# Fused sigmoid attention and ReGLU FFN: down weights in two loads with a transpose between them, long VectorE jobs behind the token pairs' joins, PSUM banks freed ahead of the token sums

## The chip, the cores and the metric

The kernel runs on one core of one Trainium2 chip. The metric is device time in microseconds (us). A run whose granted TensorE clock or time marks it as disturbed would be called slow. The granted TensorE clock that is listed with a run is its mean over the run, as a share of full speed. This mean also counts the end of the run, where TensorE has nothing left to do: in the profile of the kernel before, its last product ends at 405.11 us, and from 407.99 us to the end at 409.83 the clock is 0.50 with no work in it, which costs nothing.

## The reference

```python
# q, k, v: (8 batches, 12 heads, 448 tokens, 64), float32
scores = scale * np.matmul(q, k.transpose(0, 1, 3, 2)) - np.log(S)
attn = 1.0 / (1.0 + np.exp(-scores))                 # sigmoid, no softmax
x = np.matmul(attn, v)                               # then heads to columns: (3584, 768)
gate = np.maximum(x @ w_gate, 0.0)                   # w_gate, w_val: (768, 1536)
val = x @ w_val
out = gate * val @ w_out                             # w_out: (1536, 768), out float32
```

## The kernel before

TensorE is the engine in demand (busy 95% of the span; VectorE comes next with 69%). While it makes scores (`qk`) and attention outputs (`pv`) of batch b, the feed-forward work of earlier batches is mixed in between. Inputs of batches from 2 on come in by GpSimd's DMA queue, are relaid by VectorE (`rel`) and transposed by DMA on SyncE's queue (`qkT<-rel`). A later batch's scores cannot start before that transpose has landed: batch 3's last one is issued at 95.22 us and takes 15.9 us to land, and the scores that read it start at 111.16.

All down products, and the gate and value products from batch 2 on, are made by a seven-product scheme on two blocks of tokens (a token pair) or two batches: VectorE forms sums of the operands, TensorE makes seven products instead of eight, VectorE and ScalarE join them. A token pair of the down projection looks like this (abridged; comments are mine). In the profiles `wo` is the down weights, `T` and `S` the sums of weights and tokens, `hT` the transposed hidden activations, `u` and `y` PSUM banks in which TensorE leaves products, `ysb` the joined output, `PT` the sigmoid's output:

```python
    def weight_sums(i):                      # once, on the down weights wo = [[B11, B12], [B21, B22]]
        sub(*((T1, B12, B11), (T2, B22, T1), (B12, B22, B12), (T4, B21, T2))[i])

    def token_sums(g, p):                    # ahead of the pair
        nc.vector.tensor_tensor(out=S1, in0=A21, in1=A22, op=AOP.add)
        sub(S2, S1, A11)

    def more_token_sums(g, p):               # inside the pair
        sub(S4, A12, S2)
        sub(A21, A11, A21)                   # S3, for the fifth product; in the profile "hT<-hT"

    def down_pair(g, p, beside, then, last, first_copy):
        ...
        b, a, c = bank("u"), bank("y11"), bank("y12")        # three PSUM banks of a ring of 8
        product(b, A11, B11)
        first_copy(y1[:, lo], b)             # VectorE, or ScalarE once attention is over
        product(a, A12, B21)
        beside()                             # jobs of the step, then more_token_sums
        plus(y1[:, lo], a)
        product(b, S2, T2, False)            # adds onto b: waits for first_copy
        scaled_act(y1[:, hi], b)
        product(c, S1, T1)
        scaled_act(y2[:, hi], c)
        product(b, S3, T3, False)            # the fifth product
        plus(y2[:, hi], b)
        product(c, S4, B22, False)
        plus(y1[:, hi], c)
        store(...)
        then()                               # sums of the next piece of work
        product(b, A22, T4, False)
        scaled_act(y2[:, lo], b)
```

The two halves of the down weights are loaded together, behind a `hold`: GpSimd copies two elements of a transposed tile, so whatever it issues next waits for that transpose (in the profile the copy runs at 91.59 us, after 16.56 us of idle time that the transpose ended, and the loads are issued from 92.04 on).

```python
    def load_o():
        for i in range(2):
            cs = slice(i * NFC // 2, (i + 1) * NFC // 2)
            nc.gpsimd.dma_start(wo[:, cs, :], moe_w_out.rearrange("(c p) m -> p c m", p=P)[:, cs, :])

    def hold(b, g):
        nc.gpsimd.tensor_copy(gate[0:1, :], qkT_tiles[(b, g)][0:1, 0, 0:2])
    ...
        elif b == 2:
            hooks = {
                3: [(0, lambda: (dma_transposes(3, 0), dma_transposes(3, 1), hold(3, 1), load_o()))],
                5: [(0, lambda: (dma_transposes(3, 2), gate_sums(0, 2), gate_sums(2, 4)))],
            }
```

Of the kernel before, what the change touches and what calls it, by code (L numbers as in the profile page):

```python
# [17 lines left out]
def kernel(  # L18
# [10 lines left out]
    nc = tc.nc  # L29

    B, H, S, D = q.shape
# [3 lines left out]
    P = 128  # L35
# [123 lines left out]
    load_v(1)  # L159
    load(1, 2, 3, "kq")  # L160

    def load_o():
        for i in range(2):
            cs = slice(i * NFC // 2, (i + 1) * NFC // 2)
            nc.gpsimd.dma_start(
                wo[:, cs, :], moe_w_out.rearrange("(c p) m -> p c m", p=P)[:, cs, :]
            )

    qkT_tiles = {}
    xT_tiles = {}  # L170
# [245 lines left out]
    def more_token_sums(g, p):  # L416
        A11, A12, A21, A22 = token_blocks(g, p)
        S1, S2, S4 = sums["y"]
        sub(S4, A12, S2)
        sub(A21, A11, A21)  # L420
# [80 lines left out]
        sub(B12, B22, B12)  # L501
        sub(T4, B21, T2)

    def gv_units(g, fs, beside, first_copy, final):
        x1, x2 = xT_tiles[2 * g], xT_tiles[2 * g + 1]
        T1, T2, T4 = (late["X"][:, i] for i in range(3))
        B11, B21, T3, B22 = x1[:, 0:HD], x1[:, HD:NDC], x2[:, 0:HD], x2[:, HD:NDC]
        b, a, c = ([bank(nm) for _ in fs] for nm in ("u", "g1", "g2"))
        later((4, 5, 6, 7, 2, 3))
        gs = [[gsbp.tile([P, S], FP32, tag="gsb", name="gsb") for _ in range(3)] for _ in fs]  # L510
        sets = []
        for u, f in enumerate(fs):
            us, cols = slice(u * P, (u + 1) * P), slice(f * P, (f + 1) * P)
            S1, S2, S4 = (t[:, :, us] for t in sums["w"])
            sets.append((
                wg[:, 0:HD, cols], wg[:, HD:NDC, cols], wv[:, HD:NDC, cols],
                S1, S2, wv[:, 0:HD, cols], S4,
            ))
        del sums["w"]

        def product(ps, i, W, first=True):
            for u in range(len(fs)):
                products([(ps[u], S, HD, sets[u][i], W, first)])

        def copy(i, ps, by=nc.scalar.copy):
            for u in range(len(fs)):
                by(gs[u][i][:], ps[u][:, 0:S])  # L527

        def plus(i, ps):
            for u in range(len(fs)):  # L530
                nc.vector.tensor_tensor(  # L531
                    out=gs[u][i][:], in0=ps[u][:, 0:S], in1=gs[u][i][:], op=AOP.add
                )

        product(b, 0, B11)
        copy(0, b, first_copy)
        product(a, 1, B21)
        beside()
        plus(0, a)
        product(b, 4, T2, False)  # L540
        copy(1, b)
        product(c, 3, T1)
        copy(2, c)
        product(b, 5, T3, False)
        plus(2, b)
        product(c, 6, B22, False)
        plus(1, c)
        product(b, 2, T4, False)

        def finish(evens):  # L550
            for even in evens:
                for u in range(len(fs)):
                    if even:
                        gated(g, fs[u], 0, S, gs[u][0], b[u])
                    else:
                        gated(g, fs[u], S, S, gs[u][1], gs[u][2])

        if final == "even":
            finish((True,))
            prepare()  # L560
            return lambda: finish((False,))
        if final == "odd":
            finish((False,))
            prepare()
            finish((True,))
        else:
            finish((True, False))

    gv_queue = deque()

# [91 lines left out]

    work = deque()

    pending = []

    def push_group(g):
        if g > 0:
            work.extend([("w", g, (f, f + 1)) for f in range(0, NFC, 2)])
# [2 lines left out]
    def prepare():  # L672
        if work:
            kind, g, i = work[0]
            if kind == "w":
                unit_sums(g, i)
            elif kind == "y":
                token_sums(g, i)

    def next_work(jobs=(), alone=False):  # L680
        kind, g, i = work.popleft()

        def beside():
            while pending:
                pending.pop()()
            for job in jobs:
                job()

        if kind == "y":
            down_pair(  # L690
                g, i, lambda: (beside(), more_token_sums(g, i)), prepare, not work,
                scaled_act if alone else scaled,
            )
        else:
            first_copy = nc.scalar.copy if alone else nc.vector.tensor_copy
            if work[0][0] == "w":
                gv_units(g, i, lambda: (prepare(), beside()), first_copy, None)
            else:
                rest = gv_units(g, i, beside, first_copy, ("even", "odd")[g % 2])
                if rest:  # L700
                    pending.append(rest)

    ffn_mix(1, [(1, lambda: both(1, 0))])
    for b in range(1, B):
        if b == 1:
            cuts, pv_at = (0, 3, 6, 9, 13, 17, 21), {3: (0, 2), 5: (1, 2)}
        elif b == 2:
            cuts, pv_at = (0, 4, 7, 11, 14, 18, 21), {0: (-1, 2), 2: (0, 2), 4: (1, 2)}
        else:
            cuts, pv_at = (0, 4, 8, 12, 16, 21), {0: (-1, 2), 2: (0, 2), 4: (1, 2)}  # L710
        count = len(cuts) - 1
        hooks = {}
        if b == 1:
            mix = (3, 3, 3, 3, 3, 2)
            hooks = {
                1: [(1, lambda: both(1, 1))],
                3: [(1, lambda: both(1, 2))],
                4: [(3, lambda: dma_transposes(2, 0))],
                5: [(2, late_loads)],
            }  # L720
        elif b == 2:
            mix = (2, 2, 1, 1, 2, 1)
            hooks = {
                3: [(0, lambda: (dma_transposes(3, 0), dma_transposes(3, 1), hold(3, 1), load_o()))],
                5: [(0, lambda: (dma_transposes(3, 2), gate_sums(0, 2), gate_sums(2, 4)))],
            }
            open_late()
        elif b == 3:
            mix = (1, 1, 1, 0, 0)
            hooks = {  # L730
                0: [(0, lambda: (gate_sums(4, 6), gate_sums(6, 8)))],
                1: [(0, lambda: weight_sums(0))],
                2: [(0, lambda: (weight_sums(1), prepare()))],
            }
        else:
            mix = (0,) * count
        for m in range(count):
            jobs = []
            for i, (g, c) in enumerate(order[cuts[m] : cuts[m + 1]]):
                if m in pv_at and i == pv_at[m][1]:  # L740
                    if m == 0:
                        pv_finish(b - 1)
                        if b == 2:
                            push_group(0)
                    else:
                        pv_group(b, pv_at[m][0])
                qk_unit(b, g, c)
            if m == 0 and b > 1 and b != 3:
                jobs.append(lambda: dma_transposes(b, 2))
            if b == 3 and m == count - 2:  # L750
                jobs.append(lambda: (weight_sums(2), weight_sums(3)))
            elif b == 4 and m == 2:
                jobs.append(lambda: (gate_sums(8, 10), gate_sums(10, 12)))
            elif b == 3 and m == count - 1:
                jobs.append(lambda: (dma_transposes(4, 0), dma_transposes(4, 1)))
            elif 0 <= m - count + 2 and 3 < b < B - 1:
                jobs.append(lambda: dma_transposes(b + 1, m - count + 2))
            if b == 1:
                if m == 0:
                    load(2, 0, 1, "kq")  # L760
                    load(2, 1, 2, "kq")
                    load(2, 2, 3, "kq")
            elif m == 0 and b + 1 < B:
                if b == 3:
                    jobs.append(lambda: hold(3, 2))
                jobs.append(lambda: (load(b + 1, 0, 3, "kq"), load_v(b + 1)))
            if b % 2 and b > 2:
                if m == count - 1:
                    push_group(b // 2)
                    jobs.append(lambda: (batch_sums_t1(b // 2), batch_sums(b // 2, (0, 1))))  # L770
                    if b == B - 1:
                        jobs.append(lambda: (pv_finish(b), batch_sums(b // 2, (1, HD))))
            elif b > 3 and m == 0:
                jobs.append(lambda: batch_sums(b // 2 - 1, (1, HD)))
            if mix[m]:
                for job in jobs:
                    job()
                ffn_mix(mix[m], hooks.get(m, ()))
            else:
                next_work(jobs)  # L780
    while work:
        next_work((), True)


# [28 lines left out]
```

## Time and profile before

| | before |
|---|---|
| time, median of 4 runs | 411.29 us (411.04 to 412.12) |
| profiled span | 409.8 us |
| TensorE busy | 389.6 us |
| TensorE's waits for the last transpose of batch 3 | 4.4 us, once |
| TensorE's waits for VectorE's hT (S3) | 6.9 us in six pairs |
| mean granted clock | 0.994 in the profile, 0.990 to 0.996 over all runs |

The lines that carry the argument are in the prediction below. One more view is needed, the stretches of TensorE's clock. Its columns are the stretch and its length, then busy time and count of TensorE, its weight loads, VectorE, ScalarE and GpSimd, then the granted clock, the DMA share and GB/s:

```profile
107.62:111.03 3.41, 0.00 (x0) 0.00 (x0) 2.15 (x3) 0.89 (x3) 0.00 (x0) 1.00 0.51 66
111.03:114.44 3.41, 3.28 (x16) 1.38 (x17) 0.47 (x2) 1.85 (x4) 2.48 (x4) 0.50 0.21 11
```

A stretch of 3.41 us without any TensorE work is followed by one of the same length at clock 0.50, in which 3.28 us of work were done at half speed (six down matmuls took 2.10 us at 112.05, and 1.15 at 118.28). The two drops of the clock in this profile, at 111.03 and 407.99 us, are 87 times 3.413 us apart, so both lie on one grid of such windows. Work is compared with the clock below in windows of that length, cut at the drop of each profile, which lies elsewhere in each: in two profiles of the changed kernel at 112.17 and at 113.24 us.

### The profile page before, as it was taken

What the parts mean: (1) busy time and instruction counts of PE and PEld (TensorE: products, weight loads), DVE (VectorE), ACT (ScalarE), POOL (GpSimd) and SP (SyncE); (2) the same over time, 40 slices, a digit from 0 to 9 for tenths busy, and PEclk for the clock granted to TensorE, in tenths of its full rate; (3) what the DMA queues carried; (4) which work ended last, traced back from release to release, by engine and by line L of the source; (5) the groups of instructions that cost most, each with busy time, mean ns of one, the idle gap of its engine ahead of it and who ended that gap; (6) DMA issues with size and microseconds to landing.
All of it is one profiled execution on the core that took longest, in us unless ns stands there. A gap on an engine that the chain in (4) does not pass through costs nothing. (4 is left out here: it accounts for less than half of the span.)

```text
span 409.8 us, 8697 instructions
## 1 busy us (share of the span) xinstructions
PE 389.6 (95%) x3476; PEld 216.2 (53%) x3476; DVE 281.3 (69%) x570; ACT 229.9 (56%) x482; POOL 49.3 (12%) x74
## 2 busy tenths in 40 slices
PE   8999999999598999999999899999999899999995
PEld 3668775444244554554455445455455455555563
DVE  2443445344567789999756789999785779887662
ACT  5946777779634465655556455655645534433221
POOL 8643302301020300003000030000000000000000
PEclk9999999999999999999999999999999999999999
DMA  9999995999799791235916598022202220000235
GB/s 145 198 199 204 204 131 94 198 159 155 124 166 204 149 234 20 46 46 67 179 41 161 124 155 170 2 45 47 46 2 78 78 77 0 2 1 2 77 91 142
DMA packets 67257, 43.69 MB, mean 107 GB/s; under 512 B 35856, under 2 KB 63760, under 8 KB 67216
## 3 DMA queue, kind: packets, MB, share of 16 engines
q0 software_dynamic: 29200, 23.33, 37.3%
q1 hardware_dynamic: 37584, 19.24, 22.1%
q10 hardware_dynamic: 432, 0.56, 0.5%
q8 instruction: 27, 0.44, 0.4%
q14 instruction: 14, 0.11, 0.1%
HBM read 47.19 MB, written 11.01 MB: 142 GB/s over the span
## 5 line engine op out<-in xcount | busy, mean ns | idle before, releaser
L188 ACT ACTIVATE PT<-qk_ps 128x448 f16<-128x448 f32 (+3 forms) x318 | 150.9, 593 | 59.3 <-PE qk_ps L233 59.0
L385 PEld LDWEIGHTS <-S 128*128 128x128 f16 x576 | 56.1, 98 | 46.3 <-issue 0.4
L233 PE MATMUL qk_ps<-qkT 64*64 64x448 f16 (+2 forms) x756 | 50.6, 339 | 6.1 <-DMA qkT<-rel 4.4
L428 ACT ACTIVATE ysb<-u 128x384 f32<-128x384 f32 x32 | 15.7, 490 | 63.3 <-PE u L385 63.1
L385 PEld LDWEIGHTS <-hT 128*128 128x128 f16 x312 | 29.6, 99 | 31.6 <-DVE hT L376 9.7
L527 ACT COPY gsb<-u 128x448 f32<-128x448 f32 x48 | 25.6, 533 | 31.7 <-PE u L385 30.5
L531 DVE TENSOR_TENSOR gsb<-g,gsb 128x448 f32<-128x448 f32 x72 | 41.5, 616 | 0.1
L320 DVE SCALAR_TENSOR_TENSOR hT<-gate_sb,v_ps 128x256 f16<-128x256 f32 (+2 forms) x36 | 14.6, 420 | 37.9 <-ACT gate_sb L343 21.0
L185 DVE TENSOR_SCALAR xT<-pv_ps 128x448 f16<-128x448 f32 (+2 forms) x53 | 27.8, 566 | 16.1 <-PE pv_ps L251 15.5
L251 PE MATMUL pv_ps<-PT,v 64*64 64x448 f16 (+2 forms) x756 | 37.1, 329 | 1.0 <-issue 1.0
L385 PE MATMUL u<-wo,hT 128*128 128x384 f16 x156 | 30.7, 335 | 7.0 <-DVE hT L376 6.9
L233 PEld LDWEIGHTS <-qkT 64*64 64x64 f16 x756 | 20.1, 106 | 31.0 <-issue 17.3
L334 PE MATMUL g_ps<-xT,wg 128*128 128x256 f16 (+2 forms) x216 | 33.5, 292 | 0.1
L334 PE MATMUL v_ps<-xT,wv 128*128 128x256 f16 (+2 forms) x216 | 33.3, 291 | 0.0
L531 DVE TENSOR_TENSOR gsb<-u,gsb 128x448 f32<-128x448 f32 x36 | 21.4, 624 | 15.6 <-PE u L385 15.6
L385 PEld LDWEIGHTS <-wv 128*128 128x128 f16 x216 | 21.1, 98 | 19.8
L385 PEld LDWEIGHTS <-wg 128*128 128x128 f16 x216 | 20.3, 98 | 20.6 <-issue 3.0
L251 PEld LDWEIGHTS <-v 64*64 64x64 f16 x756 | 21.9, 107 | 12.0 <-issue 1.9
L110 POOL DMA_DIRECT2D k<-in_k_dram x14 | 10.9, 779 | 120.0 <-DVE rel L216 112.6
L334 PEld LDWEIGHTS <-wg 128*128 128x128 f16 x216 | 18.5, 97 | 11.5 <-issue 5.0
L334 PEld LDWEIGHTS <-wv 128*128 128x128 f16 x216 | 20.1, 98 | 7.6 <-DMA wv<-in_moe_w_val_dram 0.2
L385 PE MATMUL u<-xT,wg 128*128 128x448 f16 x108 | 23.5, 354 | 0.1
(71 smaller groups left out, 523.9 us busy)
## 6 DMA issues: line engine op xcount, KB each, us to landing
out_dram<-ysb SPq DMA_DIRECT2D x53, 192.0 KB, 3.0
k<-in_k_dram POOLq DMA_DIRECT2D x5, 672.0 KB, 9.3
q<-in_q_dram POOLq DMA_DIRECT2D x5, 672.0 KB, 13.3
v<-in_v_dram POOLq DMA_DIRECT2D x8, 336.0 KB, 13.3
v<-in_v_dram POOLq DMA_DIRECT2D x16, 168.0 KB, 13.3
wo<-in_moe_w_out_dram POOLq DMA_DIRECT2D x2, 1152.0 KB, 12.9
k<-in_k_dram POOLq DMA_DIRECT2D x8, 224.0 KB, 10.4
q<-in_q_dram POOLq DMA_DIRECT2D x6, 224.0 KB, 11.3
```

The lines of the kernel that those rows point to most:

```text
L110: nc.gpsimd.dma_start(t16[:, xs, cs], rows_of(src, b)[:, xs, cs])
L185: nc.vector.tensor_scalar(out=xT, in0=src, scalar1=XSCALE, scalar2=None, op0=AOP.mult)
L188: nc.scalar.activation(PT_ap, ps_ap, AF.Sigmoid, bias=sig_bias, scale=qk_scale)
L233: nc.tensor.matmul(out_of(hh)[o : o + 64, :], qkT[rows, c, cols], qkT[rows, NCH + c0 : NCH + c1, cols], start=True, stop=True, tile_positi ...
L251: nc.tensor.matmul(ps[hh][64 * r : 64 * r + 64, 0:qn], v16[rows, 2 * g + hh, c * D : (c + 1) * D], pieces[c][rows, hh, :], start=(c == 0), ...
L320: nc.vector.scalar_tensor_tensor(out=dst[:, f, a - d : z - d], in0=gate_sb[:, a - o : z - o], scalar=0.0, in1=val[:, a - o : z - o], op0=relu,
L334: nc.tensor.matmul(ps[-1][:, 0:qn], wt[:, dc, f * P : (f + 1) * P], xT_tiles[b][:, dc, q0 : q0 + qn], start=(dc == 0), stop=(dc == NDC - 1),)
L385: nc.tensor.matmul(ps[:, 0:n], A[:, k_, :], W[:, k_, :], start=(first and k_ == 0), stop=(k_ == kn - 1), skip_group_check=True,)
L428: nc.scalar.activation(o, ps[:, 0:HM], AF.Copy, scale=OUT_SCALE)
L527: by(gs[u][i][:], ps[u][:, 0:S])
L531: nc.vector.tensor_tensor(out=gs[u][i][:], in0=ps[u][:, 0:S], in1=gs[u][i][:], op=AOP.add)
```

## The change

Its intent has three parts. **Loads:** the last transpose of batch 3 shall not queue among 2.3 MB of down weights (where it took 15.9 us to land), so its relayout runs earlier, the first half of the weights is loaded ahead of it and the second half behind it. The hold that stood ahead of batch 4's inputs moves along with it. Of the weight sums, the first two that need the second half move behind the token sums. **Jobs:** relayouts and batch sums no longer stand ahead of the pair's own sums and joins in VectorE's queue. **Banks:** at the end of a gate/value unit, the gating that empties two PSUM banks comes ahead of the other half's gating and of the token sums, and nothing is deferred any more.

```diff
-    def load_o():
-        for i in range(2):
-            cs = slice(i * NFC // 2, (i + 1) * NFC // 2)
+    def load_o(i):
+        cs = slice(i * NFC // 2, (i + 1) * NFC // 2)
 ...
-    def gv_units(g, fs, beside, first_copy, final):
+    def gv_units(g, fs, beside, first_copy, then, split):
 ...
-        if final == "even":
-            finish((True,))
-            prepare()
-            return lambda: finish((False,))
-        if final == "odd":
-            finish((False,))
-            prepare()
-            finish((True,))
+        if split:
+            finish(False)
+            then()
+            finish(True)
         else:
-            finish((True, False))
+            finish(True)
+            finish(False)
+            then()
 ...
             down_pair(
-                g, i, lambda: (beside(), more_token_sums(g, i)), prepare, not work,
-                scaled_act if alone else scaled,
+                g, i, lambda: (more_token_sums(g, i), run(jobs)),
+                lambda: (run(behind), prepare()), not work, scaled_act if alone else scaled,
             )
 ...
-                3: [(0, lambda: (dma_transposes(3, 0), dma_transposes(3, 1), hold(3, 1), load_o()))],
-                5: [(0, lambda: (dma_transposes(3, 2), gate_sums(0, 2), gate_sums(2, 4)))],
+                3: [(0, lambda: (dma_transposes(3, 0), dma_transposes(3, 1), hold(3, 1), load_o(0)))],
+                5: [
+                    (1, lambda: (dma_transposes(3, 2), hold(3, 2), load_o(1))),
+                    (0, lambda: (gate_sums(0, 2), gate_sums(2, 4))),
+                ],
 ...
-                2: [(0, lambda: (weight_sums(1), prepare()))],
+                2: [(0, lambda: (prepare(), weight_sums(1), weight_sums(2)))],
 ...
-                jobs.append(lambda: (weight_sums(2), weight_sums(3)))
+                jobs.append(lambda: weight_sums(3))
 ...
-                if b == 3:
-                    jobs.append(lambda: hold(3, 2))
 ...
-                    jobs.append(lambda: (batch_sums_t1(b // 2), batch_sums(b // 2, (0, 1))))
+                    (jobs if b == B - 1 else behind).append(
+                        lambda: (batch_sums_t1(b // 2), batch_sums(b // 2, (0, 1)))
+                    )
 ...
-                jobs.append(lambda: batch_sums(b // 2 - 1, (1, HD)))
+                behind.append(lambda: batch_sums(b // 2 - 1, (1, HD)))
```

## The prediction

> **What bounds the kernel now.** I read the head of the page first, then the list of waits of TensorE alone, then the timelines of TensorE, VectorE and the DMA queues where those waits lie. The page says that TensorE works 95% of the span and the next engine 69%:
>
> ```profile
> PE 389.6 (95%) x3476; PEld 216.2 (53%) x3476; DVE 281.3 (69%) x570; ACT 229.9 (56%) x482; POOL 49.3 (12%) x74
> ```
>
> The change removes no matmul, so what it can win lies in the 20.2 us in which TensorE does nothing (409.8 less 389.6), and in matmuls that run at a reduced clock. The waits of TensorE (who waited for whom: us in total, times, longest):
>
> ```profile
> PE u L385 <- DVE hT L376: 6.9, 6, 1.7
> PE qk_ps L233 <- DMA qkT<-rel: 4.4, 1, 4.4
> ...
> PE qk_ps L233 <- DVE hT L320: 0.7, 2, 0.5
> ```
>
> The single wait of 4.4 us is for the last DMA transpose of batch 3. TensorE's timeline (start, us, what, idle before):
>
> ```profile
> 106.17 0.57 PE L233 MATMUL qk_ps<-qkT 64*64 64x448 f16 x8
> 111.16 0.96 PE L233 MATMUL qk_ps<-qkT 64*64 64x448 f16 x8 [4.42 <-DMA qkT<-rel]
> 112.05 2.10 PE L385 MATMUL u<-wo,hT 128*128 128x384 f16 x6
> ...
> 118.28 1.15 PE L385 MATMUL u<-wo,hT 128*128 128x384 f16 x6 [1.00 <-DVE hT L376]
> ```
>
> Read the durations too: six down matmuls take 2.10 us at 112.05 and 1.15 at 118.28. Windows of the same trace give a granted clock of 0.50 from 111.03 to 114.44 and 1.00 on both sides. So the wait also costs about half of 3.3 us at half clock, 1.6 us. Why the transpose is late, from DMA issues: it is issued at 95.22 and takes 15.9 us to land, where the two before it took 4.1 and 4.5. From 95 to 107 the queue is full of the two down-weight loads (1152 KB each, issued together at 92.04); from 99 to 107 the transpose's queue moves 834 small packets beside their 907[...], 104 a microsecond. Undisturbed, from 86.5 to 91, it moves 3639, some 810 a microsecond; one transpose has about 1800.
>
> The six waits of 6.9 us stand in the second half of a token pair, for the difference hT that VectorE makes for the fifth product. VectorE's timeline in the second pair shows why:
>
> ```profile
> 126.88 0.85 DVE L376 TENSOR_TENSOR X<-xT 128x1344 f16<-128x1344 f16 x1
> ...
> 128.68 0.55 DVE L376 TENSOR_TENSOR S<-hT,S 128x768 f16<-128x768 f16 x1
> 129.15 0.55 DVE L376 TENSOR_TENSOR hT<-hT 128x768 f16<-128x768 f16 x1
> ```
>
> The relayouts (rel) and batch sums (X) stand ahead of it in the queue. I measured pairs from first matmul to the next block: an undisturbed one takes 6.92 us (213.37 to 220.28). The pairs at 112.05, 124.02, 135.24, 222.99 and 233.36 take 9.26, 9.01, 7.98, 8.17 and 7.98; the one at 319.89 takes 9.97, of which 1.5 is another product. Lastly, from pv to the down pair at 205.35 takes 3.06 us where 1.81 is normal (182.89 to 184.70): the score matmuls wait for two PSUM banks that VectorE empties only after the token sums.
>
> [...]
>
> **Part 1, the loads.** The order of instructions shows that TensorE, ScalarE and SyncE keep their sequences; GpSimd gets the second load behind a copy that waits for the last transpose; VectorE's two relayout copies move ahead of one gating pair (hT/aside). They can then run at 90.97 instead of 94.47, end at 91.7, and the transpose is issued at about 91.75. Its first packets follow about 1.1 us after (85.30 to 86.4 in the trace), at 92.9. The first load, issued at 92.04 as before, moves only 39 packets up to 94.75 and is in full flow from then. The like case is the transpose at 137.73, issued beside the next batch's load: it ran fast for half a microsecond (305 packets from 139.0 to 139.5), then one for one, and took 11.0 us. So I estimate 650 to 1100 packets before 95.0, then about 116 a microsecond until the first load's 768 packets end near 101, then the rest at once. Landing near 101.7 (99 to 103.5). That is ahead of 106.7, when TensorE wants it: **the 4.4 us wait and the half clock go.**
>
> But the second load now starts only then: copy and issue 0.5 us, then about 8.9 us (2.7 us until full flow as in the first load, 6 us for 768 packets at 128 a microsecond): landing **near 111.1** (108.5 to 113), where before it was there at 108.7. TensorE would do its score units until 107.4, the first down product until 108.4, and stop there for the second, which reads the second half. Behind the landing VectorE now has two weight sums (1.3 us each) and the copy of u (0.5) ahead of the third product: 111.1 + 0.1 + 3.1 = 114.3. Then five products of 0.98 and the switch: the pair ends at 119.3, before 121.31. **Gain 2.0 us**, between 0 and 4.7. So most of what is saved in the transpose I expect to come back as a wait for weights.
>
> **Part 2, the long jobs.** With hT right behind the copy of u, the fifth product has it about 1 us before need. I replayed VectorE's queue with the durations of the trace. Losses removed against 6.92: 2.09 (124.02), 1.06, 1.25, 1.06, and 9.97 - 1.5 - 6.92 = 1.55; together 7.0. Given back: the batch sums now sit between the joins and the next sums. In the second pair they end at 8.4 us after its start, the next pair's sums at 9.5, its xT at 10.5 and the copy of u at 11.1, where TensorE needs it at 11.09: nothing to spare, 0.1 lost. Ahead of the first gate/value unit the batch sums (1.6 us) and unit sums push the copies to 0.1 to 0.2 us too late, twice: 0.3. **Net 6.6.**
>
> **Part 3, unit banks.** At 201.4 the gating that empties banks goes first: 1.25 saved; but the token sums move 1.1 us later and then the copy of u is late by about 0.3. At 299.6 the gating of the odd half (1.2 us) comes ahead of the sums where it was deferred: about 0.5 of new wait in a pair that had none. **Net 0.45.**
>
> **Sum:** 2.0 + 6.6 + 0.45 = 9.05 us; 411.3 - 9.05 = 402.3.
>
> **The rivals.**
> 1. The transpose slips nearly whole into the slow start of the load and lands by 98.5. For it: little else moves from 91 to 94.7. Then the weights are there at about 108.6, part 1 gains 4.5, and the time is 399.7. Against it: the 11 us case at 137.73.
> 2. The second load becomes the new wait in full: the transpose has a tail (before, its last packets dribbled from 109.2 to 110.3), the load lands after 112.5, and the low activity between 108 and 114 drops the clock again. Part 1 then gains nothing or loses 1; the time is 404.5 to 405.5.
> 3. VectorE becomes the bound in the gate/value stretches, where it is already busy 18.9 of 20 us (160 to 180) and 19.1 (260 to 280). Each entering delay of 1.5 us has to be worked off at some 0.5 us a unit. For it: the thin margins above. Against it: those units show no TensorE wait at all today, and only order changes, not work. It would cost 1 to 2 us: 403.5 to 404.5.
>
> **Range and chances.** The hT waits are the safest part (order alone causes them); part 1 is the widest, with 2 us either way; part 3 is small. I take 399.3 to 405.2 for 8 in 10. Faster by 2% means below 403.1, only 0.8 us above my centre: 0.6. Within 2%: 0.39. Slower by over 2% would need a stall of 17 us: 0.01.
>
> **What would show it.** Right: no TensorE wait for the transpose; no half clock near 111; the six waits for hT gone from the list; pairs of about 6.9 us at all those places but the first; a TensorE wait of some 2.5 us for the second half of the weights and about 2 us for VectorE's weight sums and copy of u; from pv to the down pair near 2.1 us at 205. Wrong: a transpose that lands before 99.5 or after 104; a second load landing before 109; half clock in the first pair; new waits of over 0.5 us at the start of gate/value stretches.

## The result, and the profile after

The changed kernel takes 405.69 us, median of 4 runs (403.46 to 407.28), where the kernel before took 411.29 (4 runs). The ratio is 0.9856, with a 95% interval of 0.9808 to 0.9905. A ratio here is the mean time of one kernel's fast runs over the mean of the other's fast runs of the same rounds, so it is not quite the ratio of the medians. The gain is 1.4%: the time lies half a microsecond above the predicted range, and the gain is 5.9 us where 9 were forecast.

Two things strike at once. The runs are spread over almost 4 us, where the kernel before, in the same rounds, stays within 1.1. And they go with the granted clock: 403.46 us at 0.996, 405.51 at 0.990, 405.87 at 0.989, 407.28 at 0.986. The profile was taken on the fastest of the four, so it shows the change at its best. The head of its page (span 401.7 us):

```profile
PE 388.8 (97%) x3476; PEld 217.2 (54%) x3476; DVE 279.9 (70%) x570; ACT 229.7 (57%) x482; POOL 49.6 (12%) x74
```

Work is as it was; of the idle time of TensorE, 20.2 us before, 12.9 are left. Its waits:

```profile
PE u L384 <- DVE ysb L422: 2.5, 3, 2.0
PE qk_ps L232 <- DMA qkT<-rel: 1.4, 1, 1.4
PE y L384 <- ACT PT L187: 1.3, 1, 1.3
```

The six waits for hT and the wait for the two PSUM banks are gone, as foretold, and so is the wait of 4.4 us. In their place stand three others. TensorE's timeline over the first pair and the second:

```profile
107.15 1.15 PE L384 MATMUL u<-wo,hT 128*128 128x384 f16 x6
109.56 1.15 PE L384 MATMUL y<-wo,hT 128*128 128x384 f16 x6 [1.26 <-ACT PT L187]
112.69 2.08 PE L384 MATMUL u<-T,S 128*128 128x384 f16 x6 [1.98 <-DVE ysb L422]
114.56 1.65 PE L384 MATMUL y<-T,S 128*128 128x384 f16 x6
...
130.21 0.57 PE L232 MATMUL qk_ps<-qkT 64*64 64x448 f16 x8 [1.44 <-DMA qkT<-rel]
```

The wait at 109.56 is put down to ScalarE, whose sigmoids ran on until 110. But the product needs the second half of the weights, which was issued at 99.74 and took 9.8 us to land, so until 109.54; and VectorE's first sum of that half starts at 109.54, released by that DMA. I take it to be the load that was waited for, as the profile itself says in most of the later runs. The next wait, 1.98 us, is for the copy of u, which stands behind two weight sums in VectorE's queue (they start at 109.54 and 110.81 us, the copy at 112.08). Then six matmuls take 2.08 us. The stretches of the clock say why:

```profile
108.76:112.17 3.41, 1.15 (x6) 0.60 (x7) 2.63 (x3) 1.24 (x3) 0.00 (x0) 1.00 1.26 204
112.17:115.58 3.41, 2.89 (x10) 1.33 (x10) 3.13 (x5) 0.49 (x1) 0.00 (x0) 0.50 1.27 205
```

TensorE worked 1.15 of 3.41 us between the two waits, and the clock went to half for the next stretch, though there was no wait as long as 3.4 us any more.

The transpose itself did better than forecast. Here are the DMA issues of the changed kernel between 91.3 and 100 us (size, median time to landing):

```profile
qkT<-rel SPq DMA_TRANSPOSE x1, 7.3
```

It took 7.3 us where it had taken 15.9. From 92.5 to 95.0 its queue started 1541 packets and the weights' queue none; the load came into full flow only afterwards (468 packets from 95 to 99 us, beside 283 of the transpose's queue). The like case of the forecast, the transpose at 137.73 us in the kernel before, went otherwise: from 140 to 147 us its queue moved 1146 packets beside 1114 of the loads', and it took 11.0 us to land.

### The profile page after: what moved, and what is told of

Read it like the earlier page. It is cut to its first block, busy times and chain, and to the rows that moved or that the text cites.

```text
span 401.7 us, 8701 instructions
## 1 busy us (share of the span) xinstructions
PE 388.8 (97%) x3476; PEld 217.2 (54%) x3476; DVE 279.9 (70%) x570; ACT 229.7 (57%) x482; POOL 49.6 (12%) x74
## 4 chain that ended last, share of the span: by engine, by line
PE 86%; DMA 6%; DVE 3%; ACT 3%; issue 1%; ACTq 0%; POOL 0%; POOLq 0%
PE u L384 33%; PE g L384 15%; PE y L384 9%; PE qk_ps L232 7%; PE g_ps L333 6%; PE pv_ps L250 6%; PE v_ps L333 6%; DMA qkT<-rel 3%; DMA wo<-in_moe_w_out_dram 2%; ACT PT L187 2%; PE warm_ps L175 1%; PE trt L201 1%; DVE hT L319 1%; DVE xT L184 1%; ACT ysb L427 1%
## 5 line engine op out<-in xcount | busy, mean ns | idle before, releaser
L384 PE MATMUL u<-wo,hT 128*128 128x384 f16 x156 | 29.7, 326 | 0.1
L110 POOL DMA_DIRECT2D k<-in_k_dram x14 | 10.9, 780 | 126.5 <-DVE rel L215 119.3
L333 PEld LDWEIGHTS <-wg 128*128 128x128 f16 x216 | 18.5, 98 | 11.5 <-issue 5.0
L333 PEld LDWEIGHTS <-wv 128*128 128x128 f16 x216 | 20.2, 98 | 7.4
L444 DVE SCALAR_TENSOR_TENSOR ysb<-u,ysb 128x384 f32<-128x384 f32 x14 | 7.8, 558 | 23.1 <-ACT ysb L427 14.0
```

Source lines behind the costliest of these rows:

```text
L110: nc.gpsimd.dma_start(t16[:, xs, cs], rows_of(src, b)[:, xs, cs])
L333: nc.tensor.matmul(ps[-1][:, 0:qn], wt[:, dc, f * P : (f + 1) * P], xT_tiles[b][:, dc, q0 : q0 + qn], start=(dc == 0), stop=(dc == NDC - 1),)
L384: nc.tensor.matmul(ps[:, 0:n], A[:, k_, :], W[:, k_, :], start=(first and k_ == 0), stop=(k_ == kn - 1), skip_group_check=True,)
L444: nc.vector.scalar_tensor_tensor(out=o, in0=ps[:, 0:HM], scalar=OUT_SCALE, in1=o, op0=AOP.mult, op1=AOP.add)
```

## The experiments

Twelve kernels ran, all correct. Each of the three groups of four shared a chip and 11 runs of the kernel before (means 411.65, 411.54 and 411.53 us).

### The changed kernel again (a_again)

No edit.

> The changed kernel again, unaltered, to see how its time is spread. Theory (the clock): TensorE is only a third busy from 108.3 to 112.7 us (two waits with six matmuls between them), and [...]one, two or three windows of 3.4 us at half clock follow, 1.7 us each; then the runs lie at 403.4, 405.2 and 407 us with granted clocks near 0.996, 0.990 and 0.986. Rival (the transfers): the second weight load or the transpose lands at a different time from run to run; then times spread continuously while the granted clock stays put.

Measured: 405.79 us (404.89 to 406.54, 4 runs), ratio 0.9856 (0.984 to 0.9872), granted clock 0.996 once and 0.989 three times. The result stands. In this profile the second half of the weights came later (waits of TensorE), and the window behind the wait is again one at half clock (stretches of the clock, cut on this profile's own grid):

```profile
PE y L384 <- DMA wo<-in_moe_w_out_dram: 2.3, 1, 2.3
```

```profile
109.82:113.24 3.42, 1.15 (x6) 0.60 (x7) 2.42 (x2) 0.43 (x1) 0.00 (x0) 1.00 1.26 205
113.24:116.65 3.41, 2.69 (x9) 1.31 (x9) 3.34 (x6) 0.49 (x1) 0.00 (x0) 0.50 1.27 206
```

So both theories have something: the load's landing varies by a microsecond between runs (the second product starts at 110.84 us here, at 109.56 in the first profile), and the clock varies too (405.05 and 406.54 us came at the same 0.989). The next experiment separates them.

### TensorE kept busy in the two waits (a_warm)

```diff
+        dummies(7)           # first pair only: c[:, 0:HM] <- wg, wg, start and stop; c is written anew later
         product(a, A12, B21)
 ...
+        dummies(11)
         product(b, S2, T2, False)
```

> The changed kernel with 7 matmuls whose result is thrown away ahead of the second down product of the first token pair and 11 ahead of the third, about as long as the two waits there (1.1 and 1.8 us), so TensorE stays busy without the waits being any shorter. Theory (the clock): no half-clock window near 112 us in the profile, granted clock 0.998 or more, all runs within about 0.5 us of each other, near 401.8 us (403.5 of the best run less 1.6). Rival (the transfers, or a slow state of the chip): the spread and the median near 405.5 us stay.

Measured: 403.17 us (402.54 to 404.05, 4 runs), ratio 0.9795 (0.9782 to 0.9807); granted clock 0.996 or 0.997 in every run. The stretches of its clock:

```profile
110.05:113.46 3.41, 1.92 (x12) 1.17 (x12) 1.94 (x2) 0.11 (x1) 0.00 (x0) 1.00 1.26 205
113.46:116.87 3.41, 3.20 (x21) 1.84 (x19) 3.41 (x6) 0.54 (x2) 0.00 (x0) 1.00 1.27 205
...
400.18:402.27 2.09, 0.00 (x0) 0.00 (x0) 0.00 (x0) 0.00 (x0) 0.00 (x0) 0.50 0.26 90
```

No useful work was added and no wait for another engine was shortened; in this profile the load even came later (TensorE's second product starts at 111.54 us, not at 109.56), and the thrown-away matmuls bridge only part of that wait. Still the mean falls by 2.5 us against a_again (405.75 to 403.23). **The half clock costs the changed kernel about 2.5 us on average**, some 0.8 us more or less by the two intervals, and more than the one window of the profile can cost. The clocks point the same way (0.9968 against 0.9907 on average), but they can't be turned into an exact sum: all that this profile lacks of a full clock is the idle 2.09 us at its end (last line), and the profile of a_again has no such end. The theory was right in the cause and not in the numbers: it had 401.8 us, a spread of 0.5 us and a clock of 0.998, where 403.2, 1.5 and 0.997 came. The spread that is left is of the size of the load's variation; that it comes from the load isn't shown.

### The loads' part alone (p1_loads)

The hunks of the loads, the hold and the weight sums from the diff above, on the kernel before.

> The kernel before with the loads' part alone: two loads with the last transpose between, and the weight sums in the new order. Theory: the 4.4 us wait for the transpose goes, but the waits for the second half and for VectorE (about 1.3 and 2 us) and half-clock windows stand in its place, so only 0 to 2 us are gained: 409.3 to 411.3 us, with a spread of 2 us or more and a granted clock of 0.985 to 0.995. Rival (this part is the whole gain, as the name of the change puts it first): 405 to 406 us.

Measured: 410.37 us (409.42 to 412.28, 6 runs), ratio 0.9972 (0.9953 to 0.9991): 1.1 us gained, as the theory had it. The rival falls. Its profile shows a whole 6.8 us at half clock:

```profile
106.20:109.61 3.41, 1.75 (x14) 0.61 (x9) 1.26 (x4) 3.41 (x8) 0.00 (x0) 1.00 1.20 208
109.61:113.02 3.41, 2.33 (x7) 1.00 (x8) 3.38 (x4) 0.05 (x1) 0.00 (x0) 0.50 1.26 205
113.02:116.43 3.41, 3.41 (x12) 1.67 (x11) 2.38 (x4) 0.49 (x1) 0.00 (x0) 0.50 1.27 205
```

TensorE was busy 1.75 of 3.41 us before the drop, and the clock stayed at half for a second window, where the first throttled one held a wait too (2.33 us of work; the throttled windows of after and a_again, with 2.89 and 2.69 us, were followed by full clock). So two waits of 1 to 2 us cost more clock here (6.83 us at half clock) than the one wait of 4.4 us with full work behind it in the kernel before (3.41 us).

### The price of the half clock in the kernel before (b_warm)

```diff
+        if (b, g, c) == (3, 2, 0):           # 26 thrown-away matmuls, just ahead of the late scores
+            for _ in range(26):
+                nc.tensor.matmul(ps[0][:, 0:HM], wg[:, 0, 0:P], wg[:, 0, 0:HM], start=True, stop=True, ...)
         qk(qkT_tiles[(b, g)], c, 0, NCH, lambda hh: ps[hh][:, 0:S])
```

> The kernel before with 26 matmuls whose result is thrown away in its 4.4 us wait for the transpose, the wait itself unchanged. It measures the price of the half clock by itself. Theory: no half-clock window near 111 us, granted clock 0.996 to 0.999, 1.6 us faster than before: 409.7 us. Rival (the clock costs nothing that the wait does not already cost): 411.3 us as before.

Measured: 410.39 us (410.04 to 410.75, 5 runs), ratio 0.9966 (0.9953 to 0.9979): 1.3 us by the means, 1.6 expected; granted clock 0.997 to 1.0. In the kernel before, the half clock behind the long wait is worth about 1.3 us, half of what it is worth in the changed kernel.

### The long jobs alone (p2_jobs)

The `jobs`/`behind` hunks on the kernel before.

> The kernel before with the long VectorE jobs alone moved behind the joins (loads and gating order as before). Theory: the six waits for hT go (1.0, 2.1, 1.1, 1.25, 1.1 and 1.55 us), 1.4 us come back as a wait for the first transpose of batch 4, whose relayout now stands a microsecond later while the pair is two shorter: about 6.5 us gained, 405.1 us, with the 4.4 us wait for the last transpose of batch 3 still there and a granted clock as before (0.991 to 0.995). Rival (VectorE becomes the bound, the waits come back elsewhere): less than 4 us gained, 407.6 us or more.

Measured: 405.80 us (405.23 to 406.22, 4 runs), ratio 0.9865 (0.9841 to 0.9889). **This part alone brings as much as the whole change.** The rival falls. The waits for hT are gone; what is left in its waits is two transposes, the old one of 4.6 us and a new one of 1.7:

```profile
PE qk_ps L233 <- DMA qkT<-rel: 6.3, 2, 4.6
```

### The banks alone (p3_banks)

The gating order of `gv_units` on the kernel before.

> The kernel before with the gating order alone changed (banks freed ahead of the token sums, none deferred). Theory: 1.25 us saved before the pair near 205 us, 0.4 us given back in it and 0.4 us in the pair near 302 us, where the copy of u comes late: 0.5 us gained, 411.1 us. Rival (the token sums' delay costs as much as the banks bring): 411.6 us, no change.

Measured: 411.29 us (408.66 to 412.22, 6 runs), ratio 0.9986 (0.9961 to 1.0012). The interval holds both theories; the time settles nothing. The profile shows the exchange: the wait for the banks is gone, and two waits for the copy of u, 0.5 us together, are there.

```profile
PE u L385 <- DVE ysb L423: 0.5, 2, 0.2
```

### Both weight loads together, with the early relayout (a_nohold)

```diff
-  3: ... hold(3, 1), load_o(0)
+  3: ... hold(3, 1), load_o(0), load_o(1)
-  5: (1, lambda: (dma_transposes(3, 2), hold(3, 2), load_o(1)))
+  5: (1, lambda: dma_transposes(3, 2))
```

> The changed kernel, but with both weight loads issued together, as before; only the earlier relayout of the last transpose is kept. Theory (the hold between the loads is what makes the second half late: it gives the second load its own slow start): the transpose still lands before 104 us, since most of its packets go out before the loads are in full flow, the second half is there by 108.7 us or earlier, the wait for it is under 0.5 us and the time falls by 1 to 2.5 us, to 403.5 to 404.8 us. Rival (the hold is needed, the transpose starves as before): a wait of 2 us or more for the transpose, and 407 us or more.

Measured: 403.71 us (400.63 to 404.20, 6 runs), ratio 0.9799 (0.9772 to 0.9826). The rival falls: with nothing between the loads the transpose lands in 7.5 us (7.3 with the hold, 15.9 in the kernel before), for the early relayout alone gets it out of the weights' way.

```profile
qkT<-rel SPq DMA_TRANSPOSE x1, 7.5
```

The theory is right in the time and not in the wait: 1.39 us were still waited for the second half, where I had expected under 0.5. Over five profiles that keep the hold (after, a_again, a_warm, a_both, a_trans) the second product starts at 109.6 to 111.5 us, 110.6 on average; here at 109.8. So the earlier load explains some 0.8 us, on single profiles. The rest goes with a higher mean clock (0.9943 against 0.9907), of which the idle end of the run may be a part; this profile still has one window at half clock, behind one with 1.43 us of work. In full flow the DMA engines move some 200 GB/s in all these profiles (203 to 208 in the stretches around the first pair); whether a still earlier load would gain more was not tried. Without the hold, batch 4's inputs too are issued earlier (93.55 us).

### Copy of u by ScalarE, and the first transpose of batch 4 a step earlier (a_both)

```diff
-        first_copy(y1[:, lo], b)
+        (scaled_act if (g, p) == (0, 0) else first_copy)(y1[:, lo], b)
 ...
                 jobs.append(lambda: weight_sums(3))
+                behind.append(lambda: dma_transposes(4, 0))
 ...
-                jobs.append(lambda: (dma_transposes(4, 0), dma_transposes(4, 1)))
+                jobs.append(lambda: dma_transposes(4, 1))
```

> The changed kernel with two touches: in the first token pair u is copied by ScalarE, not VectorE, so the third product does not stand behind two weight sums; and the first transpose of batch 4 is started one step earlier, behind the first pair's joins. Theory: the 2.0 us wait for the copy falls to 0.4 us, the 1.4 us wait for the transpose goes, and with less idle time half-clock windows become fewer: 405.8 less 1.6, less 1.4, less up to 2 for the clock: 401 to 402.8 us. Rival (the second load is the bound of that stretch and what is saved behind it is lost to another wait): 404 us or more.

Measured: 402.49 us (400.22 to 403.07, 5 runs), ratio 0.9767 (0.9741 to 0.9793). Both waits are gone, and the wait for the load stays. So does one window at half clock (111.20 to 114.61 us, behind one with 1.18 us of work):

```profile
PE y L384 <- DMA wo<-in_moe_w_out_dram: 2.2, 1, 2.2
```

### The changed kernel without its loads' part (a_noloads)

The loads' hunks taken back, the jobs and the banks kept.

> The changed kernel with its loads' part undone (both loads together, relayout of the last transpose late, weight sums in the old order); the long jobs and the banks as changed. Theory (the loads' part nets nothing: what it saves in the 4.4 us wait it loses in two waits and more half clock): 405 to 406 us, as the changed kernel, with a 4.5 us wait for the transpose in the profile. Rival (the parts add up: 1.2 us from the loads alone): 407 us.

Measured: 405.21 us (404.11 to 406.54, 5 runs), ratio 0.9859 (0.9835 to 0.9884), where the whole change has 0.9856. So **the loads' part, in company with the others, nets nothing**. The long wait is back in the profile (and the 1.4 us in the second pair beside it), and it costs no more than what stood in its place:

```profile
PE qk_ps L233 <- DMA qkT<-rel: 5.7, 2, 4.3
```

### The first transpose of batch 4 a step earlier (a_trans)

The second half of the edit of a_both alone.

> The changed kernel with the first transpose of batch 4 started one step earlier, behind the first pair's joins. Theory: the 1.44 us wait for it in the second pair goes and nothing takes its place: 1.4 us faster than the changed kernel, 404.3 us. Rival (the relayouts behind the first pair push the token sums of the second): a wait of 0.5 us or more for VectorE in the second pair, 405 us or more.

Measured: 403.17 us (400.59 to 405.58, 6 runs), ratio 0.9791 (0.9755 to 0.9827). The 1.44 us wait is gone, nothing replaced it, and the gain against a_again is about 2.6 us by the medians; more than the wait, since the mean clock of these six runs happened to be higher too (0.9935). The six runs show the clock's part most plainly: two at 0.998 and 0.999 took 400.88 and 400.59 us, four at 0.991 took 402.90 to 405.58. (These four, at one clock, still lie 2.7 us apart; what parts them isn't shown.) The profile is of one of the four:

```profile
108.45:111.86 3.41, 1.27 (x7) 0.60 (x7) 1.30 (x2) 1.83 (x5) 0.00 (x0) 1.00 1.24 204
111.86:115.27 3.41, 1.56 (x6) 0.70 (x6) 3.41 (x6) 0.00 (x0) 0.00 (x0) 0.50 1.27 206
115.27:118.69 3.42, 3.42 (x12) 1.60 (x11) 1.05 (x2) 0.98 (x2) 0.00 (x0) 0.50 1.26 203
```

The same kernel, without any edit, pays the half clock in some runs and hardly in others.

### All three touches (a_best), and with thrown-away matmuls (a_bestwarm)

The edits of a_nohold and a_both together; a_bestwarm adds 9 and 1 thrown-away matmuls at the two places of a_warm.

> The changed kernel with three touches: both weight loads together (only the earlier relayout kept), u of the first pair copied by ScalarE, the first transpose of batch 4 a step earlier. Theory: what the three brought singly adds up less what they share in the half clock: waits of about 1.4 us for the second half and 0.4 us for its sum are all that is left in the first pair; 400 to 401.5 us. Rival (they share all): 402.5 us, as with two of them.

> The same with 9 thrown-away matmuls ahead of the second down product and 1 ahead of the third. Theory (the clock): a granted clock of 0.997 or more in all runs and about 1 us less than without them, 399.5 to 400.5 us. Rival (so short a wait drops no clock): no gain, or up to 0.5 us lost where the thrown-away matmuls outlast the wait.

Measured: a_best 399.21 us (398.87 to 400.26, 4 runs), ratio 0.9706 (0.9682 to 0.973), granted clock 0.998 to 1.0. a_bestwarm 399.07 us (398.98 to 400.49, 4 runs), ratio 0.9706 (0.9681 to 0.9731). The rival is right for a_bestwarm: with waits of 1.2 and 0.24 us no clock was lost in the first place (the only half clock in the profile of a_best is the idle 1.29 us at its end), so there was nothing to gain. For a_best the three touches brought more than I expected. Its stretches of the clock, and its two waits in the first pair:

```profile
107.05:110.47 3.42, 2.22 (x23) 0.94 (x22) 1.75 (x5) 2.98 (x8) 0.00 (x0) 1.00 1.22 206
110.47:113.88 3.41, 3.17 (x18) 1.55 (x18) 3.41 (x4) 1.49 (x4) 0.00 (x0) 1.00 1.26 205
```

```profile
PE y L384 <- DMA wo<-in_moe_w_out_dram: 1.2, 1, 1.2
...
PE u L384 <- DVE T L375: 0.2, 1, 0.2
```

a_best beats both kernels: 2.9% below the one before, some 6 us below the changed one.

## Why the prediction was wrong, point by point

**The bound, and where time could be won:** right. TensorE stayed the bound, and all that was won or lost lies in its waits and its clock.

**Part 1, "the 4.4 us wait and the half clock go":** this is the step that failed. The wait went, by a transpose that landed after 7.3 us instead of the forecast 10 (at 98.8 us, near the first rival's 98.5). The half clock did not go. I had assumed that a drop takes a window without any work, as at 111.03 us in the kernel before (0.00 us of work from 107.62 to 111.03); that was not shown, and the other drop of the same profile, at 407.99, follows a window with 0.53 us of work. So I left my own two waits of 2.5 and 2 us out of the clock's account, since neither is 3.4 us long, and named the drop only in the second rival, whose other half, a load after 112.5 us, didn't come. The runs showed half clock behind windows with 1.15 of 3.41 us of work (after, a_again), and a second window of it where the first throttled one held a wait too (1.56 us of work in a_trans, 2.33 in p1_loads). Price: 2.5 us on average (a_warm against a_again). So the gain of part 1, forecast as 2.0 us, was 1.1 alone (p1_loads) and nothing in company (a_noloads). Within the first pair the waits themselves were near the forecast: about 1.3 to 2.3 us for the load and 1.98 for the copy, where I had 2.5 and 2. That the first pair of the profile ends at 119.06 us, forecast 119.3, is luck: the load came 1.6 us earlier than forecast, and the half clock took about as much; in a_again the pair ends at 120.23.

**The size of the range for part 1** was meant to hold this (0 to 4.7); but only its low end came true, and with the next point the sum left the range.

**Part 2, net 6.6 us:** right in its mechanism, off in size. All six waits went. Alone it gained 5.6 us (ratio 0.9865 on 411.54). The missing piece is that I replayed VectorE's queue for TensorE's next product, the next sums and the next copy, but not for the DMA transpose that the same relayouts feed. In the second pair the relayout now starts 2.6 us into the pair where it started 1.7 us into it, the pair is 2 us shorter, and the scores of batch 4 wait 1.44 us for the transpose. Moving that transpose up removes the wait (a_trans). The thin margins that I did work out (0.1 and 0.3 us) held: the list of waits shows none at the start of a gate/value stretch, so the third rival is refuted.

**Part 3, net 0.45 us:** the exchange is in the profile as described (1.25 us saved, two late copies of u). The two late copies cost 0.4 us in the pair near 200 us (7.32 against 6.93) and 0.37 in the pair near 295, so the size was about right. The time of p3_banks cannot tell it from nothing.

**The sum:** 9.05 was forecast, 5.9 came. The half clock (2.5 us that were not in the sum) and the second pair's transpose (1.44) more than account for the gap of 3.2; in the other direction the transpose and the second load were earlier than forecast (the second product at 110.6 on average over the five profiles, forecast 111.2). How the parts share between them is not settled to less than half a microsecond: alone they gain 1.1, 5.6 and 0.6, which is 1.4 more than they gain together, and of this 1.0 is the wait for hT in the first pair, which the loads' part and the jobs' part both remove.

**What stays open:** the second load lands anywhere between 109.5 and 111.5 us in profiles with the hold. Most of this is settled by the traces: GpSimd issues it behind a copy that waits for the transpose, and that lands after 7.3 to 8.5 us, so the issue lies between 99.74 and 101.14 us; from there it takes 9.6 to 9.8 us in five of the six profiles (with p1_loads), and 11.5 in a_warm. So in these profiles the hold handed the delay of the transpose on to the load. In all of them the load begins slowly: from 101.25 to 101.5 us the DMA engines move 55 to 142 GB/s, where full flow is some 200, and in the first profile the weights' queue starts 100 packets between 101 and 102.5 us (by the 445 packets of 102.5 to 106 us, I estimate full flow at about 190 in that time); what sets the length of that start, and of the transpose, was not tested. Nor was it pinned down at how much work the clock drops, and busy time alone doesn't decide it: drops followed windows with 0.00 to 1.75 us of work, and a_warm and a_best had windows of 1.92 and 2.22 without one; but the kernel before has a window with as little as the 1.75 of p1_loads, and the kernel after one with 1.50 near its end, and the clock of the window behind each is 1.00 (first line from before, second from after; the count of busy time may not be what the clock goes by).

```profile
128.10:131.51 3.41, 1.75 (x11) 1.09 (x12) 2.22 (x7) 0.49 (x1) 0.00 (x0) 1.00 1.10 167
...
395.48:398.89 3.41, 1.50 (x10) 0.69 (x7) 0.75 (x2) 0.49 (x1) 0.00 (x0) 1.00 0.54 115
```

## What to carry to other kernels

When a long wait of the bounding engine is replaced by two short ones, add up the work in each window of about 3.4 us, not the length of each wait: windows that were one third busy (1.15 us) dropped the clock here as a full stop did, and how many windows at half clock follow varies (one in after and a_again, two in a_trans and p1_loads). When a job is moved behind others in one engine's queue, follow every consumer of what it makes, a DMA and what that feeds included (here scores that waited 1.44 us). And before putting a transfer between two others, look at whether issuing it earlier is enough: here the transpose took 7.5 and 9.2 us to land with the early relayout and no hold (a_nohold, a_best), 7.3 to 8.5 with it, and 15.9 and 16.1 with neither (before, p2_jobs); the hold brought nothing that a run shows.
